# Transposed gathers by DMA from ScalarE, and VectorE's low parts moved in the attention steps

## Chip, cores and metric

One core of a Trainium2 chip runs the whole kernel as one program. The metric is device time in microseconds (us) of one execution; several executions are timed and their median is given. TensorE is called PE, VectorE DVE, ScalarE ACT, GpSimd POOL and SyncE SP, as in the profile.

## What is computed

Linear attention over 8 batches, 8 heads, 576 positions and 64 dimensions, with features exp(±(x·w_phi − max)), followed by two mixture-of-experts layers over the 4608 token rows of 512 numbers, each row going to one of 8 experts:

```python
num = np.einsum('bhsf,bhfd->bhsd', q_p, kv)
den = np.einsum('bhsf,bhf->bhs', q_p, z)[..., None] + 1e-06
...
e_idx = np.argmax(logits, axis=1)
...
h = np.maximum(x[mask] @ w1[e], 0.0)
out[mask] = gate_w[mask, None] * (h @ w2[e])
```

The second layer does the same with other weights and a sigmoid factor on its output.

## The kernel before

Float32 numbers are carried as two float16 parts, a high part `hi` and a low part `lo` (the rest), so that matrix products of float32 quality run as three float16 products on PE. ACT usually makes the high part, DVE the low part.

**Order.** The program is written for a manual schedule: each engine runs its instructions in the order of the Python code. Small chains of DVE work (`Weave`) are put in between, a few steps at each call of `weave.step`.

**Attention.** The loop over `t` has 9 steps for each of the 8 batches, and 6 more; a step is `t % 9`. The work of different batches and heads is staggered: `at(lag)` gives the (batch, index) that began `lag` steps earlier. A step projects keys and queries (PE), takes maxima `km` and `nm` and the difference `kd` (DVE, L1319, L1276, L1325), makes exponentials (ACT, L1334, L1405), the products `kv` (PE, L1348) and `num` (PE, L1433), and normalizes `num` into `xt` (`norm`, DVE, L1413 to L1417), which frees the PSUM bank of `num`. For each finished batch the rows of the next layer are written tile by tile: `x_hi` (ACT, L1515) one step, `x_lo` (DVE, L1520) the step after, `a_T` (PE, L424, eight transposes into the bank `px`, the first four of the high part), `x_logits` and a table entry (`x_enter`, L405, and `tab_out`, L410). Beside this `split0` splits the weights of the first block: `load`, `mx`, `scale`, `hi` (ACT, L249), `lo` (DVE, L258) and `store`, each set down for a step number by `job`; `split_step(split, weave, t, what)` runs all jobs of a kind up to `t`.

**Experts.** `run` is a generator over 80 tiles of 128 rows, 40 of the first block and 40 of the second. For each tile a gather (POOL, `gather`, L788) brings its rows from DRAM to one of four buffers `xg`; `x_T` transposes them, `first` is the first layer in two halves (PE, L818 to L820), `hidden` makes its high part (ACT, L829) and low part (DVE, L830), `second` is the second layer (PE, L840 to L842). In the first block the result `y` of the tile is then scaled (`y_max`, `y_scale`), split (`y_hi` on ACT, L887; `y_lo` on DVE, L892), transposed on PE (`y_T`, L424, copied by ACT at L902) and routed for the second block. The weights of the second block are split meanwhile (L229, L233, L249, L258).

**Transposes of gathered rows.** `x_T(n, i, pe)` has two ways. With `pe` it is eight transposes on PE into a PSUM bank (L424, `px` or `pl` `<-ident,xg`) and a copy to `xT` (`x_T_out`, L807, by ACT at the end of a step). Without, it is one DMA transpose (L800), issued by SP at the top of the step. Which way is taken is set in `run` for the tile two ahead: `soon` is true for all tiles of the first block, so these go to PE, and most of the second block's take the DMA. `lazy` puts PE's transposes behind those of `y` near the end of the step.

**From attention to experts.** `tiles()` advances `run` by one stage. At the end of the attention a few stages are drawn in among the last table entries. When the last entry is in, `route_a` and `route_b` compute on DVE which expert's rows stand in which tile; the gathers of the fourth tile and later need that.

Of the kernel before, what the change touches and what calls it, by code (L numbers as in the profile page):

```python
# [23 lines left out]
B, H, S, D = 8, 8, 576, 64  # L24
# [18 lines left out]
E = 3  # L43
# [13 lines left out]
def attention_two_moe(  # L57
# [6 lines left out]
    nc = tc.nc  # L64
# [85 lines left out]
    def done(chain):  # L150

        while True:
            try:
                next(chain)
            except StopIteration as e:
                return e.value
# [137 lines left out]
    def split_step(split, weave, t, what):  # L294

        if what == "scale":
            split.chains = [weave.add(c) for c in split.go(t, what)]
        else:
            if what == "hi":
                for c in split.chains:  # L300
                    weave.finish(c)
            split.go(t, what)
# [119 lines left out]
    def transposes(ps, parts):  # L422
        for i, a in enumerate(parts):
            nc.tensor.transpose(ps[:, i, :], a, ident16)  # L424
# [15 lines left out]
    def view(t, dt, start, *dims):  # L440
        a = t.bitcast(dt) if dt != F32 else t
        n = int(np.prod(dims))
        names = "abcd"[: len(dims)]
        return a[:, start : start + n].rearrange(
            f"p ({' '.join(names)}) -> p {' '.join(names)}", **dict(zip(names[1:], dims[1:])))
# [18 lines left out]
    xTb = [view(xT_m[i], F16, 0, 8, 128) for i in range(2)]  # L464
# [313 lines left out]
    def xg(n, i):  # L778
        return xgb[(i + state.get("shift", 0)) % 4]
# [12 lines left out]
    def pt():  # L792
        state["pts"] += 1
        return bank(state["pt"][state["pts"] % len(state["pt"])], F16, 8, 128)

    def x_T(n, i, pe=False):

        hl = xg(n, i)[:, 0:DM].bitcast(F16)
        if not pe:
            nc.sync.dma_start_transpose(out=xTb[i % 2], in_=hl)  # L800
            return
        xTp[n, i] = pt()
        transposes(xTp[n, i], [hl[:, 128 * k : 128 * k + 128] for k in range(8)])
# [177 lines left out]
    def run(seq):  # L981
# [3 lines left out]
        head = seq[0][1] == 0  # L985

        def at(u):
            return seq[u] if 0 <= u < n0 else None
# [40 lines left out]
        for u in range(n0 + 3):  # L1029
            cur, nxt_ = at(u), at(u + 1)  # L1030
# [10 lines left out]

            pre = head and cur and cur[1] == E - 1

            soon = pre or cur and head and at(u + 2) and at(u + 2)[0] == 0

            turn = head and at(u + 2) and at(u + 2)[0] == 1 and at(u + 2)[1] < 2
            if at(u + 2) and known(u + 2) and not soon and not turn:
# [31 lines left out]
            elif old2:  # L1079
                i = old2[1]  # L1080
# [88 lines left out]
    with ExitStack() as actx:  # L1169
# [14 lines left out]
        weave = Weave()  # L1184

        split0 = Splitter(0, stage0, parts_of(*xg_m, *xT_m), sm, ((), ()), 32, 3, 7, junk=acc.tile([128, 1024], F8, name="junk"))
# [299 lines left out]
        def x_of(b, c):  # L1486
            return xts[b][:, c] if c < 4 else xrs[b // 2]
# [30 lines left out]
        def x_lo(b, c):  # L1518
            hl = row(b, c)[:, 0:DM].bitcast(F16)
            nc.vector.scalar_tensor_tensor(  # L1520
                out=hl[:, DM : 2 * DM], in0=x_of(b, c), scalar=rows[b, "s"][:, c : c + 1], in1=hl[:, 0:DM],
                op0=ALU.mult, op1=ALU.subtract)
# [60 lines left out]
        def x_hots(b):  # L1583
            n = 4 + b % 2
            if b < B - 2:
                areas = [wop.tile([128, 1024], F32, tag="wo", name="wo")]
            else:
                areas = [io.tile([128, 4, 2, F], F32, tag="kprem", name="kprem", bufs=1).rearrange("p a b c -> p (a b c)")]
            mems = []
            for a in areas:  # L1590
                a = a if a.dtype == F16 else a.bitcast(F16)
                mems += [a[:, 416 * i : 416 * i + 416] for i in range(a.shape[1] // 416)]
            mems = mems[0:4]
            if n == 5:
                mems.append(wk.tile([128, 8, 128], F16, tag="xT", name="xT", bufs=1).rearrange("p a b -> p (a b)")[:, 0:416])
            at_ = []
            pk, po = rows.pop((b, "pk"))
            yield from hots(at_, pk, po, codes[0][:, 9 * (b // 2) + 4 * (b % 2) :], mems)
            rows[b, "hots"] = at_[0]

        def x_enter(b, tag="qf"):
            rows[b, "pt"] = tab_add(tag, rows.pop((b, "hots")))
# [22 lines left out]
        def tiles():  # L1625
            if not chains.get("route"):
                chains["route"] = next(experts)

        chains = {}
        for t in range(9 * B + 6):  # L1630
            b, s = t // 9, t % 9

            def at(lag, n=9):

                u = t - lag
                return (u // 9, u % 9) if 0 <= u < 9 * B and u % 9 < (n if n else 4 + u // 9 % 2) else None
# [15 lines left out]
            def end(lag, name):  # L1652
                if at(lag, 1):
                    weave.finish(chains.pop((name, at(lag, 1)[0])))

            if 9 <= t < 18 or t >= 9 * B - 14:
                next(zeros_, None)
            if t == 4:
# [61 lines left out]
                    done(q_parts(0))  # L1720
                weave.step()
            done(norm_)
            if at(17, 0) and at(17)[0] < B - 1:
                x_lo(*at(17))
            each(6, x_max)
            weave.step()

# [35 lines left out]
            split_step(split0, weave, t, "hi")  # L1763
            weave.step(2)
            weave.step()
            split_step(split0, weave, t, "lo")
            if entered is not None:
                tab_out(0, rows.pop((entered, "pt")))
            weave.step()
# [60 lines left out]
        x_store(last)  # L1830
        done(x_places(last))
        done(x_hots(last))
        x_enter(last, "num2")
        tab_out(0, rows.pop((last, "pt")))

# [89 lines left out]
```

## Time and profile before

| | us |
|---|---|
| median of 3 runs | 1468.89 |
| range of these | 1467.31 to 1476.05 |
| the profiled execution | 1468.27 |
| its span in the trace | 1466.4 |

The profiled execution has a span from the first to the last instruction; times in the trace count from its start. "Busy" is the time in which an engine had an instruction running. Matmuls overlap each other, so the distance between the starts of two is what one costs in a full PE. "Idle before <- releaser" says how long an engine stood before an instruction, and what ended the wait. The granted clock is 1.00 at 2.4 GHz and 0.50 at 1.2 GHz.

### The profile page before, as it was taken

How to read it: one execution, taken by the hardware profiler on the slowest of the kernel's cores; microseconds unless marked ns; L12 is line 12 of the kernel's file. 1: busy time of each engine (PE TensorE's matmuls, PEld its weight loads, DVE VectorE, ACT ScalarE, POOL GpSimd, SP SyncE). 2: the span in 40 equal slices, each digit the busy share in tenths (PEclk: the TensorE clock that was granted, in tenths of full speed). 3: DMA queues.
4: the chain of work that ended last, by engine and by line, in shares of the span. 5: the costliest groups of instructions: out<-in, count | busy, mean ns of one | idle time of the engine just before them, and what ended most of it. 6: DMA issues, size and time to landing. Idle time of an engine off the chain costs nothing. (4 is left out here: it accounts for less than half of the span.)

```text
span 1466.4 us, 40153 instructions
## 1 busy us (share of the span) xinstructions
PE 1407.8 (96%) x16132; PEld 1146.3 (78%) x16132; DVE 852.2 (58%) x2579; ACT 649.7 (44%) x1010; POOL 159.4 (11%) x208
## 2 busy tenths in 40 slices
PE   6999999999899998999999999999999999999997
PEld 4999888989889896777777777777676777777775
DVE  3688888887887757687777877775611111111110
ACT  1467666666657541456565555643211111111111
POOL 1000000000000000111111111011121212121211
PEclk8999999999898888999999999999999999999999
DMA  7367767768563272466667665789454262773470
GB/s 232 130 207 260 245 195 244 217 215 242 200 206 132 112 290 81 122 231 235 224 214 239 228 224 198 228 309 368 168 143 129 77 192 68 231 240 95 128 248 32
DMA packets 157681, 285.31 MB, mean 195 GB/s; under 512 B 85657, under 2 KB 86573, under 8 KB 150320
## 3 DMA queue, kind: packets, MB, share of 16 engines
q1 hardware_dynamic: 143104, 241.10, 50.6%
q0 software_dynamic: 12352, 41.40, 8.6%
q8 instruction: 130, 2.13, 0.6%
q14 instruction: 63, 0.52, 0.1%
q10 hardware_dynamic: 2032, 0.16, 0.1%
HBM read 444.04 MB, written 98.63 MB: 370 GB/s over the span
## 5 line engine op out<-in xcount | busy, mean ns | idle before, releaser
L830 DVE SCALAR_TENSOR_TENSOR qs<-proj,qs 128x512 f16<-128x512 f32 x107 | 73.6, 688 | 246.3 <-ACT qs L829 245.6
L818 PE MATMUL proj<-xT,w 128*128 128x128 f16 x896 | 154.1, 220 | 0.0
L819 PE MATMUL proj<-xT,w 128*128 128x128 f16 x896 | 154.0, 220 | 0.0
L820 PE MATMUL proj<-xT,w 128*128 128x128 f16 x896 | 154.0, 220 | 0.0
L1433 PE MATMUL num<-kvsb,E 128*128 128x65 f32 x1024 | 130.3, 283 | 10.4 <-DVE xt L1417 9.6
L819 PE MATMUL proj<-xT,v 128*128 128x128 f16 x816 | 138.7, 219 | 0.1
L820 PE MATMUL proj<-xT,v 128*128 128x128 f16 x816 | 138.7, 219 | 0.0
L818 PE MATMUL proj<-xT,v 128*128 128x128 f16 x816 | 138.7, 219 | 0.0
L1348 PE MATMUL kv<-v,kp 128*128 128x128 f32 x1024 | 138.4, 292 | 0.0
L1433 PEld LDWEIGHTS num<-kvsb,E 128*128 128x128 f32 x1024 | 126.4, 201 | 13.1 <-issue 7.8
L818 PEld LDWEIGHTS <-w 128*128 128x128 f16 x1344 | 132.4, 99 | 2.0
L819 PEld LDWEIGHTS <-w 128*128 128x128 f16 x1344 | 132.4, 99 | 2.0
L820 PEld LDWEIGHTS <-w 128*128 128x128 f16 x1344 | 132.4, 98 | 0.0
L1348 PEld LDWEIGHTS kv<-v,kp 128*128 128x128 f32 x1024 | 129.5, 205 | 0.4 <-issue 0.4
L841 PE MATMUL num<-w,qs 128*128 128x512 f16 x336 | 127.3, 379 | 0.0
L842 PE MATMUL num<-w,qs 128*128 128x512 f16 x336 | 127.3, 379 | 0.0
L840 PE MATMUL num<-w,qs 128*128 128x512 f16 x336 | 127.3, 379 | 0.0
L829 ACT ACTIVATE qs<-proj 128x512 f16<-128x512 f32 x107 | 63.5, 594 | 141.1 <-PE proj L820 138.0
L842 PEld LDWEIGHTS <-qs 128*128 128x128 f16 x640 | 62.6, 98 | 75.5
L819 PEld LDWEIGHTS <-v 128*128 128x128 f16 x1216 | 118.9, 98 | 2.5 <-issue 0.3
L818 PEld LDWEIGHTS <-v 128*128 128x128 f16 x1216 | 118.9, 98 | 2.1
L820 PEld LDWEIGHTS <-v 128*128 128x128 f16 x1216 | 118.9, 98 | 0.0
(358 smaller groups left out, 3636.0 us busy)
## 6 DMA issues: line engine op xcount, KB each, us to landing
w<-pl SPq DMA_DIRECT2D x152, 1024.0 KB
v<-pl SPq DMA_DIRECT2D x80, 1024.0 KB
ks<-pl SPq DMA_DIRECT2D x80, 1024.0 KB
pl<-wo SPq DMA_DIRECT2D x66, 512.0 KB
w<-in_moe_w_dram SPq DMA_DIRECT2D x64, 512.0 KB
wf<-in_moe_w_dram SPq DMA_DIRECT2D x64, 512.0 KB
pl<-qs SPq DMA_DIRECT2D x26, 512.0 KB
ks<-in_k_dram SPq DMA_DIRECT2D x16, 576.0 KB
```

The costliest lines, as they stand in the source:

```text
L818: nc.tensor.matmul(h[:, j], wk[:, 0, cs], xT[:, k], start=(k == 0), stop=False)
L819: nc.tensor.matmul(h[:, j], wk[:, 0, cs], xT[:, 4 + k], start=False, stop=False)
L820: nc.tensor.matmul(h[:, j], wk[:, 1, cs], xT[:, k], start=False, stop=(k == 3))
L829: nc.scalar.activation(out=hi, in_=h, func=AF.Relu)
L830: nc.vector.scalar_tensor_tensor(out=lo, in0=h, scalar=0.0, in1=hi, op0=ALU.max, op1=ALU.subtract)
L840: nc.tensor.matmul(y, h[:, 0, k], wk[:, 0], start=(k == 0), stop=False)
L841: nc.tensor.matmul(y, h[:, 0, k], wk[:, 1], start=False, stop=False)
L842: nc.tensor.matmul(y, h[:, 1, k], wk[:, 0], start=False, stop=(k == 7))
L1348: nc.tensor.matmul(ps[:, half, h % 2], kp[:, c, half, :], vw(v1, 4 * h + c), start=(h % 2 == 0 and half == 0 and c == 0), stop=False)
L1433: nc.tensor.matmul(ps[:, c, 0:V], e[:, half, 128 * c : 128 * c + 128], kw(g, half), start=(half == 0), stop=(half == 1))
```

## The change

Gathered rows are transposed by DMA in the first block too, from tile 6 on (the seventh); every DMA transpose is now issued by ACT in place of SP. In an attention step `x_lo` is called at the top, ahead of all else, in place of after `done(norm_)`. The split's `lo` jobs are run at the top of the next step in steps without an `x_hi`, and where they were in the others. Before the last table entry one more stage of the experts is drawn.

```diff
-            nc.sync.dma_start_transpose(out=xTb[i % 2], in_=hl)
+            nc.scalar.dma_start_transpose(out=xTb[i % 2], in_=hl)
...
-            soon = pre or cur and head and at(u + 2) and at(u + 2)[0] == 0
+            soon = pre or cur and head and at(u + 2) and at(u + 2)[0] == 0 and at(u + 2)[1] < E + 3
...
+            if at(17, 0) and at(17)[0] < B - 1:
+                x_lo(*at(17))
+            split_step(split0, weave, t - 1, "lo")
             if 9 <= t < 18 or t >= 9 * B - 14:
                 next(zeros_, None)
...
             done(norm_)
-            if at(17, 0) and at(17)[0] < B - 1:
-                x_lo(*at(17))
             each(6, x_max)
...
-            split_step(split0, weave, t, "lo")
+            if not (at(16, 0) and at(16)[0] < B - 1):
+                split_step(split0, weave, t - 1 if t < 9 * B + 5 else t, "lo")
+            else:
+                split_step(split0, weave, t, "lo")
...
         done(x_hots(last))
+        tiles()
         x_enter(last, "num2")
```

On ACT, one tile of the first block before, from the high part of y (L887) on; `wf` are weights of the second block, `px` and `pl` PSUM banks, numbers behind a name tell buffers apart:

```order
L887 ACTIVATE qs_146<-num_7448,cs 128x512
L829 ACTIVATE qs_147<-kv 128x512
L249 ACTIVATE wo<-wf_6790,sb 128x1024
L233 ACTIVATE junk,wmx<-wf_6791 128x1024
L829 ACTIVATE qs_147<-proj 128x512
L902 COPY xT_144<-px 128x1024
L807 COPY xT_143<-pl 128x1024
L249 ACTIVATE qs_145<-wf_6790,sb 128x1024
L233 ACTIVATE junk,wmx<-wf_6791 128x1024
L887 ACTIVATE rw_6786<-num,cs 128x512
```

The same tile on ACT now:

```order
L887 ACTIVATE qs_146<-num_7448,cs 128x512
L829 ACTIVATE qs_147<-kv 128x512
L249 ACTIVATE wo<-wf_6859,sb 128x1024
L233 ACTIVATE junk,wmx<-wf_6860 128x1024
L829 ACTIVATE qs_147<-proj 128x512
L902 COPY xT_144<-px 128x1024
L800 DMA_TRANSPOSE xT_144<-xg_142 128x8x128
L249 ACTIVATE qs_145<-wf_6859,sb 128x1024
L233 ACTIVATE junk,wmx<-wf_6860 128x1024
L887 ACTIVATE rw_6855<-num,cs 128x512
```

The copy of the gathered rows' transposes (L807) went, and the DMA transpose (L800) stands in its place, ahead of the next tile's L249, L233 and L887. There are 34 more DMA transposes than before, and SP has none.

On DVE, an attention step with an `x_lo` (L1520, `rows_f<-xt`), before, from the split's low part of the step ahead to that of this step:

```order
L258 SCALAR_TENSOR_TENSOR xT_144<-w_1_153,sb,xT_144 128x1024
L1413 TENSOR_SCALAR den<-num 128x4
L1415 RECIPROCAL den<-den 128x4
L1319 TENSOR_REDUCE km<-proj 128x4
L1417 TENSOR_TENSOR xt<-num,den 128x4x64
L1276 TENSOR_REDUCE nm<-proj 128x4
L1325 TENSOR_TENSOR kd<-proj,km 128x512
L1520 SCALAR_TENSOR_TENSOR rows_f<-xt,sb,rows_f 128x512
L229 TENSOR_REDUCE wmx<-w_0_152 128x1
L258 SCALAR_TENSOR_TENSOR wo<-w_0_154,sb,wo 128x2x512
```

The same step on DVE now:

```order
L258 SCALAR_TENSOR_TENSOR xT_144<-w_1_153,sb,xT_144 128x1024
L1520 SCALAR_TENSOR_TENSOR rows_f<-xt,sb,rows_f 128x512
L1413 TENSOR_SCALAR den<-num 128x4
L1415 RECIPROCAL den<-den 128x4
L1319 TENSOR_REDUCE km<-proj 128x4
L1417 TENSOR_TENSOR xt<-num,den 128x4x64
L1276 TENSOR_REDUCE nm<-proj 128x4
L1325 TENSOR_TENSOR kd<-proj,km 128x512
L229 TENSOR_REDUCE wmx<-w_0_152 128x1
L258 SCALAR_TENSOR_TENSOR wo<-w_0_154,sb,wo 128x2x512
```

`x_lo` moved ahead of six instructions, those that normalize `num` and read the projections.

On DVE at the end of the attention, where the last one-hot rows (L396) are followed by the table add (L410), the start of `route_a` (L668, L671) and the scaling of a tile's y (L870 to L892), before:

```order
L396 TENSOR_SCALAR xT<-iota_c,po 128x288
L410 TENSOR_TENSOR tab_94<-tab_94,num_6762 96x384
L668 TENSOR_TENSOR v_0_150<-nxt_111,row_115 128x8
L671 TENSOR_TENSOR v_0_150<-v_0_150,iota_t 128x288
...
L870 TENSOR_TENSOR c<-xg_141,efac_169 128x1
L872 TENSOR_REDUCE mx<-num 128x1
```

The same place now:

```order
L396 TENSOR_SCALAR xT<-iota_c,po 128x288
L870 TENSOR_TENSOR c<-xg_141,efac_169 128x1
L872 TENSOR_REDUCE mx<-num 128x1
...
L892 SCALAR_TENSOR_TENSOR qs_146<-num,cs,qs_146 128x512
...
L830 SCALAR_TENSOR_TENSOR qs_145<-kv,qs_145 128x512
L410 TENSOR_TENSOR tab_94<-tab_94,num_6831 96x384
L668 TENSOR_TENSOR v_0_150<-nxt_111,row_115 128x8
```

The scaling and splitting of that y and one low part of a hidden layer (L830) now stand ahead of the table add and the routing.

## Rows read from the trace of the kernel before

**Rows 1.** Page, part 2: granted clock of PE in 40 equal slices.
```profile
PEclk8999999999898888999999999999999999999999
```

**Rows 2.** Windows of the attention and the first block: us, busy by engine, clock, DMA, GB/s.
```profile
core 0: us, PE busy (x) PEld busy (x) DVE busy (x) ACT busy (x) POOL busy (x), PEclk, DMA share, GB/s
100.00:545.00 445.00, 417.34 (x4548) 395.21 (x4547) 353.20 (x934) 285.58 (x473) 15.45 (x20) 0.91 0.65 213
603.00:1041.00 438.00, 437.86 (x5492) 332.94 (x5490) 321.55 (x1117) 237.73 (x333) 51.68 (x63) 1.00 0.70 240
```

**Rows 3.** Timeline of PE in the first block: start us, us, instruction; four tiles apart.
```profile
780.24 0.38 PE L840 MATMUL num<-w,qs 128*128 128x512 f16 x1
...
803.28 0.61 PE L424 MATMUL px<-ident,qs 128*128 128x128 f16 x8
803.73 0.61 PE L424 MATMUL pl<-ident,xg 128*128 128x128 f16 x8
804.17 0.38 PE L840 MATMUL num<-w,qs 128*128 128x512 f16 x1
...
827.57 0.38 PE L840 MATMUL num<-w,qs 128*128 128x512 f16 x1
```

**Rows 4.** Gathers in mid-block and at its end, DMA transposes: times to landing, of issue.
```profile
DMA to landing us min/median/max: 3.8/5.4/6.4
...
xg<-x_d,eidx POOLq DMA_INDIRECT x3, 8.0
...
L800 SPq DMA_TRANSPOSE xT<-xg x36: 1244/1261/3014, 1033.6 to 1427.5; - x36
```

**Rows 5.** Timelines of POOL, ACT, DVE and PE in one tile of the first block.
```profile
851.22 1.03 POOL L788 DMA_INDIRECT xg<-x_d,idx  x1 [10.01 <-PE pl L424]
...
853.39 1.03 ACT L807 COPY xT<-px 128x1024 f16<-128x1024 f16 x1
854.29 1.18 ACT L249 ACTIVATE qs<-wf,sb 128x1024 f16<-128x1024 f32 x1
...
859.23 0.69 ACT L887 ACTIVATE qs<-num,cs 128x512 f16<-128x512 f32 x1 [2.73 <-DVE cs L881]
...
860.50 0.74 DVE L892 SCALAR_TENSOR_TENSOR qs<-num,cs,qs 128x512 f16<-128x512 f32 x1
...
862.24 0.22 PE L424 MATMUL pl<-ident,qs 128*128 128x128 f16 x1
```

**Rows 6.** Waits of PE (100 to 545 us) and DVE (100 to 500): total, times, longest.
```profile
PE num L1433 <- DVE xt L1417: 9.0, 11, 1.7
PE px L424 <- DVE rows_f L1520: 8.3, 5, 2.2
...
PE px L424 <- DVE pb L192: 4.1, 2, 2.0
...
DVE km L1319 <- PE proj L1256: 45.6, 35, 2.4
```

**Rows 7.** Timelines of DVE and PE in the attention step shown above.
```profile
195.81 0.15 DVE L1413 TENSOR_SCALAR den<-num 128x4 f32<-128x4 f32 x1
...
196.67 0.41 DVE L1417 TENSOR_TENSOR xt<-num,den 128x256 f32<-128x256 f32 x1
...
198.20 0.74 DVE L1520 SCALAR_TENSOR_TENSOR rows_f<-xt,sb,rows_f 128x512 f16<-128x512 f32 x1
...
199.00 0.61 PE L424 MATMUL px<-ident,rows_f 128*128 128x128 f16 x4 [2.21 <-DVE rows_f L1520]
```

**Rows 8.** Windows of 4 us behind four such waits, columns as in rows 2.
```profile
200.00:204.00 4.00, 4.00 (x24) 3.87 (x25) 1.74 (x5) 2.02 (x3) 0.00 (x0) 0.50 0.40 116
268.00:272.00 4.00, 4.00 (x28) 3.64 (x29) 2.12 (x7) 1.61 (x3) 0.00 (x0) 0.50 0.68 215
332.00:336.00 4.00, 4.00 (x29) 3.64 (x29) 2.26 (x7) 2.80 (x6) 0.91 (x1) 0.50 0.50 133
464.00:468.00 4.00, 4.00 (x22) 3.93 (x21) 3.82 (x6) 3.19 (x6) 0.00 (x0) 0.50 0.00 0
```

**Rows 9.** Timeline of PE where attention ends and the first block begins.
```profile
569.10 0.26 PE L405 MATMUL num<-kprem 128*96 128x128 f16 x1 [2.11 <-DVE kprem L396]
...
590.40 0.29 PE L424 MATMUL px<-ident,xg 128*128 128x128 f16 x2 [0.22 <-DMA xg<-x_d,idx]
```

## Prediction

> **What bounds the kernel now.** I read the page's busy shares and slices first, then the windows by stage, PE's waits in each stage, and last the timelines of one tile and of one attention step. The page's line of granted clocks has an 8 in slice 1, then in slices 11 and 13 to 16 (of 36.7 us each), and 9 from there on [rows 1]. The windows [rows 2] split that. In the attention (100 to 545 us) PE is busy 417 of 445 us, but at a mean clock of 0.91, while DVE is busy 79% and ACT 64%. In the first mixture-of-experts block (603 to 1041 us) PE is busy 437.86 of 438 us at clock 1.00: there only work taken from PE shortens anything. In that stretch the list of PE's waits is empty.
>
> A tile of the first block shows what is in it [rows 3]: 8 transposes of y begin at 803.28, 8 of the gathered rows (px or pl<-ident,xg) at 803.73, the second layer at 804.17. Four tiles take 827.57 − 780.24 = 47.33 us, 11.83 each.
>
> **The change part by part.**
>
> *1. Transposes leave PE.* From tile 6 to tile 39 of the first block, 34 tiles lose their 8 transposes: 804.17 − 803.73 = 0.44 us each [rows 3], since in a full PE the start-to-start time is the price, not the 0.61 us that the row shows. 34 × 0.44 = 15.0 us. The Trainium skill (TensorE: Matmul & The Clock Gate, Part 4) gives about 275 ns for a transpose within a kernel, 2.2 us a tile; by it 75 us would go. The rows disagree: eight fit between 803.73 and 804.17, 55 ns each, and the sum keeps these.
>
> *2. ACT issues the transfer.* ACT loses a 1.03 us copy of the transposed rows (PSUM to SBUF) and gets the issue of a DMA transpose. No row shows one on ACT; on SP it took 1.244 to 3.014 us, median 1.261 [rows 4]. I take 1.26: about +0.2 us on an engine that is not full. The new thing is a wait: the issue stands in ACT's order at the top of the step, right behind the copy of y's transposes, and needs the gather of that tile to have landed. Queued behind it are two operations for the second block's weights (L249, L233) and then y_hi (L887), on which y_lo on DVE and then PE's transposes of y wait.
>
> Is the gather late? One tile [rows 5]: the gather starts at 851.22, and one takes 3.8 to 6.4 us to landing, median 5.4 [rows 4], so 856.6. ACT comes to that place at 853.39, stands 3.2 us, issues until 857.9, then needs the 2.2 us from 854.29 to 856.50 (2.73 before 859.23) for L249 and L233: 860.1 against y_hi at 859.23. It counts 0.44 more, as PE reaches the next tile that much earlier: 1.3 us late. Two covers: DVE starts y_lo only at 860.50, so y_hi (0.69) may be about 0.6 late; and y_lo ends at 861.24, 1.0 before PE's transposes of y at 862.24. 1.6 of cover for 1.3: nothing is lost. With the slowest gather, 6.4, 0.7 is. ACT idles 2.73 in this tile; over the stretch it is 438 − 237.7 = 200 us [rows 2], 5.4 for each of some 37 tiles, so the other three of a group of four have more. One tile in four may lose up to 0.7, 8 times: 0 to +6, I take +1. It cannot gain.
>
> *3. The DMA engines.* They are 0.70 busy in this stretch at 240 GB/s [rows 2], which makes 343 when full; 128 × 1024 two-byte numbers are 0.26 MB, estimated at 0.8 us of all engines, 0.07 of a tile. Free room is 0.30, and the transposed rows are needed a step later. I take 0. The Trainium skill (Trainium Kernel Development and Optimization, Key Constraints) says that DMAs of all queues share the 16 engines and another issuer saves only issue time. By it the transfer's 0.8 us would still be 0 here with 0.30 free, and a loss where the engines are full; that case is a rival below.
>
> *4. The second block* already had its transposes as transfers, from SP; all come from ACT now, 36 that ran [rows 4]. SP loses that issue. ACT issues at the top of a step, when the gather has long landed and the next hidden layer is 48 matmuls of 55 ns away, 2.65 us. 0; at most a few tenths either way.
>
> *5. x_lo first in the attention step.* PE's waits there [rows 6]: 8.3 us in 5 plus 4.1 in 2 for a step whose second four transposes of a rows tile (L424) need x_lo (L1520), 12.4 us in 7, one a batch. (The two put down to pb are the same: x_lo ends beside it.) In the one shown [rows 7] x_lo starts at 198.20, behind six instructions of DVE, and PE goes on at 199.00. Now x_lo starts where den did, 195.81, and ends by 196.55; PE has its transposes done by about 197.2. What is late next is xt (L1417), which frees the bank that the following num matmuls write: 196.67 + 0.41, and now 0.74 later, so 197.8. A wait of 0.6 to 0.7 stays of 2.2. 7 × 0.7 = 5 of 12.4 remain: −7.5. Bounds: −12.4 (all goes), and 0 (xt later takes it all).
>
> *6. The clock.* Behind that wait the granted clock is 0.50 from 200 to 204: 1.2 in place of 2.4 GHz. The same stands behind those of three other batches, at 268, 332 and 464 us [rows 8]. Each such stretch is some 7 us long, so it costs about 3.4 us; 4 × 3.4 = 13.6. As a wait of 0.7 stays in the same step, I count half as gone: −7. Bounds 0 and −13.6.
>
> *7. x_lo in the other steps, and low parts of the weights a little later.* The 24 other x_lo steps of the seven batches put 0.74 us ahead of km and xt. DVE waits 45.6 us for PE before km in 100 to 500 us, 35 times [rows 6], so in most steps x_lo fills that gap. Where it does not, num's wait for xt (9.0 us in 11) grows. The split's low parts only move past a few short operations. I take +3, bounds −3 to +8.
>
> *8. One more stage of the experts ahead of the last table entry.* The wait of 2.11 us at 569.10 is filled with 2.65 us of matmuls. But the table add and the routing chain now stand behind y_max, y_lo and one hidden low part on DVE, and their end releases the gather for which PE waits 0.22 at 590.40 with no slack [rows 9]. So only what the moved work finds of idle DVE time ahead of the table add comes through. −1, between −2.1 and, if the chain ends later, +2.
>
> **Sum.** −15.0 + 1 − 7.5 − 7 + 3 − 1 = −26.5. The profiled execution took 1468.27 us (span 1466.4 and 1.9 around it), 0.6 under the median of three, 1468.89. 1468.3 − 26.5 = 1441.8, as a median about 1442.
>
> **The rivals.**
>
> A. *The attention gives nothing*: xt takes over x_lo's wait and the clock falls as before. For it: DVE is 79% busy, and num already waits for xt 11 times. Against: DVE's 45.6 us of idle time. Then −15 + 1 − 1: 1453.5.
>
> B. *The transfers become the bound* of the first block: were the engines full, each would push the weights by 0.8 us, 34 × 0.8 = +27. For it: 0.70 is a mean, and the weights come in bursts; against: it leaves 0.30 free. 1468.3 − 15 + 27 − 12.5 = 1468, no change.
>
> C. *ACT stands too long behind the gather*, slower than before. The three gathers at the stage's end took 8.0 us [rows 4]. At 8.0 the tile of rows 5 gets y_hi at 862.7, 3.5 late, 3.9 with the shift, 2.3 beyond its cover. The other three of a group have about 2.4 us more idle and two of them thinner cover; I work them at 0.5 to 1.5, mean over the four 1.3. 34 × (1.3 − 0.44) = +29, less 12.5 from the attention: 1485. It decides from a landing of about 7.3 us on, where 0.8 us a tile eats everything. Against: no gather in mid-block took over 6.4.
>
> D. *The clock stays up wherever x_lo was late*: all of 12.4 and 13.6 goes: 1468.3 − 15 + 1 − 26 − 1 = 1427.
>
> **How the numbers follow.** Forecast 0.64, A 0.20, B 0.05, C 0.06, D 0.05. A measurement of this kernel can tell about 1% from no change; 1% under the median is 1454.2. A lies on that line: a little over half below, as its own bounds go down further than up. Faster: 0.64 + 0.05 + 0.11 = 0.80; same: 0.09 + 0.05 = 0.14; slower: 0.06. The range goes from 1426, by D with a gain in part 7, to 1458, A with the full +6 of part 2.
>
> **What would show it.** In the profile after: no px or pl<-ident,xg from the seventh tile on, four tiles in about 45.6 us (−1.77), PE's waits in 603 to 1030 still empty, a DMA transpose on ACT of about 1.3 us, ACT idle before it for the gather by 1 to 4 us, y_hi later but y's transposes not waiting. In the attention: 7 waits at L424 gone, waits of about 0.7 at L1433 behind them, mean clock 0.93 or 0.94. Wrong it would be if PE waits for y_lo at L424 in the first block (C), for weights at L818 or L840 (B), or if the attention is as long as before (A).

## The result, and the profile after

The changed kernel takes 1481.41 us (median of 20 runs, 1472.54 to 1493.27) against 1464.41 us before (20 runs, 1457.47 to 1476.05): a ratio of 1.0113, 95% interval [1.0091, 1.0135]. It is slower by 1.1%, where 1442 and faster was forecast. The profiled execution has a span of 1477.5 us against 1466.4.

The two halves of the change came out apart, one far better than forecast and the other far worse. To see it, the span is cut at the starts of tiles: a tile starts with the first of its second layer's 24 matmuls (L840, as the first and last line of [rows 3]). The starts are numbered from 0 in the trace's order, and two tiles whose second layers follow each other closely share one: start 1 is that of the second and third tile, start 40 that of two tiles of the second block. So start 2 belongs to the fourth tile, and start 39 to the first tile of the second block. "Tile 2" or "tiles 2 to 39" in the expectations and below mean these starts.

| stretch, us | before | after | difference |
|---|---|---|---|
| beginning to start 0 (attention, change-over) | 561.42 | 532.30 | −29.1 |
| start 0 to 2 | 41.80 | 40.16 | −1.6 |
| start 2 to 39 (first block) | 437.75 | 468.08 | +30.3 |
| start 39 to 41 (change of block) | 37.76 | 45.62 | +7.9 |
| start 41 to the end (second block) | 387.67 | 391.34 | +3.7 |

First the page's line of clocks and the windows, columns as in [rows 2]. The second window ends at start 0.

```profile
PEclk9999999999999799999999999999999999999999
```

```profile
100.00:545.00 445.00, 426.01 (x4896) 400.51 (x4895) 372.90 (x1018) 291.33 (x484) 15.13 (x22) 0.95 0.68 220
100.00:532.30 432.30, 413.92 (x4758) 391.76 (x4757) 363.21 (x968) 289.32 (x480) 14.65 (x20) 0.94 0.68 222
603.00:1041.00 438.00, 404.72 (x4862) 300.28 (x4860) 305.37 (x1055) 190.89 (x274) 48.09 (x58) 0.98 0.79 248
```

The same stretch of before, 100 us to start 0:

```profile
100.00:561.42 461.42, 431.44 (x4761) 408.35 (x4760) 364.00 (x968) 291.21 (x481) 15.45 (x20) 0.90 0.64 208
```

In the attention, 11.6 of the 29.1 us are idle time gone (461.42 − 431.44 = 30.0 against 18.4), and 17.5 are busy time of PE that shrank with the same instructions in it: the clock, 0.90 to 0.94. The dips in slices 11 to 16 of [rows 1] are gone; one 7 remains.

In the first block PE is idle 33.3 us of 438 where it was idle 0.14, at clock 0.98. Its waits, and ACT's (total, times, longest), 600 to 1040 us:

```profile
PE qf L429 <- ACT xT L902: 17.8, 7, 3.6
PE px L424 <- DVE rw L892: 5.3, 4, 1.4
PE pl L424 <- DVE qs L892: 4.1, 3, 1.4
PE kv L818 <- DMA w<-pl: 1.5, 1, 1.5
...
ACT wo L249 <- issue: 52.5, 9, 8.9
ACT os L934 <- issue: 40.0, 8, 5.5
ACT junk L233 <- DMA wf<-in_moe_w_dram: 39.9, 7, 6.6
...
ACT qs L249 <- issue: 23.0, 5, 7.0
```

PE never waits for the transposed rows. It waits for y_lo (L892) at y's transposes, and for ACT's copy of them (L902), each time behind a late ACT. ACT waits, 115.5 us in 22, for "issue" ahead of L249 and L934, the instructions that stand right behind the transfer. The name means that no finished instruction explains the wait; the timelines of four tiles do: in 26 of 31 tiles ACT issues the transfer within 0.2 us of the landing of that tile's gather. First POOL, ACT, DVE:

```profile
750.02 1.03 POOL L788 DMA_INDIRECT xg<-x_d,idx  x1 [9.85 <-DVE gs L316]
...
763.62 1.06 POOL L788 DMA_INDIRECT xg<-x_d,idx  x1 [4.59 <-DVE po L373]
774.74 1.02 POOL L788 DMA_INDIRECT xg<-x_d,idx  x1 [10.06 <-DVE c L914]
...
789.51 1.03 POOL L788 DMA_INDIRECT xg<-x_d,idx  x1 [11.91 <-DVE val L896]
```

```profile
755.05 1.52 ACTq L800 DMA_TRANSPOSE xT<-xg  x1
756.62 0.20 ACT L934 ACTIVATE os<-os 128x4 f32<-128x4 f32 x1 [4.75 <-issue]
...
760.78 0.69 ACT L887 ACTIVATE qs<-num,cs 128x512 f16<-128x512 f32 x1 [0.48 <-DVE cs L881]
...
770.37 1.25 ACTq L800 DMA_TRANSPOSE xT<-xg  x1
771.66 1.15 ACT L249 ACTIVATE wo<-wf,sb 128x1024 f16<-128x1024 f32 x1 [6.88 <-issue]
772.72 0.67 ACT L887 ACTIVATE qs<-num,cs 128x512 f16<-128x512 f32 x1
...
780.50 1.06 ACT L233 ACTIVATE junk<-wf 128x1024 fp8e5<-128x1024 f32 x1 [5.59 <-DMA wf<-in_moe_w_dram]
780.75 1.36 ACTq L800 DMA_TRANSPOSE xT<-xg  x1
...
782.03 1.00 ACT L902 COPY xT<-pl 128x1024 f16<-128x1024 f16 x1
```

```profile
756.85 0.17 DVE L936 TENSOR_SCALAR os<-os 128x4 f32<-128x4 f32 x1 [3.00 <-ACT os L934]
...
762.48 0.74 DVE L892 SCALAR_TENSOR_TENSOR qs<-num,cs,qs 128x512 f16<-128x512 f32 x1
...
773.61 0.74 DVE L892 SCALAR_TENSOR_TENSOR qs<-num,cs,qs 128x512 f16<-128x512 f32 x1
```

Read them as one chain: gather at 763.62, landed when L800 starts at 770.37; ACT, which was idle for 6.88 us up to L249 (the last 1.29 are the issue), goes on with L249 and y_hi (772.72); y_lo on DVE (773.61); and when its last reads of the old row buffer are done (L895, L896), the next gather starts, 774.74. Then it begins again. The stand makes the gather late, and the late gather makes the next stand. PE's own work for four tiles, without the transposes, is 45.55 us, 11.4 for each. The plain round, 763.62 to 774.74, takes 11.12 and would still fit. The rounds beside it do not: 13.60 us from 750.02, where the gate's L934 stands behind the transfer and DVE waits 3.00 us for it, and 14.77 from 774.74 to the next gather at 789.51, where ACT waits 5.59 us for the weights `wf`.

Those weights are late by a second path. SP's loads wait for ACT's transfers, too, which they never did before; the sum in 600 to 1030 us, and SP's issues around the transfer of 770.37:

```profile
SPq L482 <- DMA xT<-xg: 116.1, 18, 11.4
```

```profile
762.73 1.15 SPq L262 DMA_DIRECT2D pl<-qs  x1
773.62 0.61 SPq L482 DMA_DIRECT2D v<-pl  x2
...
775.33 0.40 SPq L222 DMA_DIRECT2D wf<-in_moe_w_dram  x1
```

The load at 773.62 had waited for a semaphore (a counter on which engines wait) that the transfer raises when it lands, so it stood behind a transfer that ACT had not even issued; `wf` went out after it. PE's largest wait, L429 for ACT's copy (17.8 us in 7), comes each time right behind one of ACT's seven waits for `wf`. In PE's timeline:

```profile
739.04 0.38 PE L840 MATMUL num<-w,qs 128*128 128x512 f16 x1
...
783.09 0.27 PE L429 MATMUL qf<-wg,xT 128*128 128x32 f16 x4 [2.38 <-ACT xT L902]
...
790.71 0.38 PE L840 MATMUL num<-w,qs 128*128 128x512 f16 x1
```

Four tiles in 51.67 us, against 47.33 in [rows 3].

### The profile page after: what moved, and what is told of

The parts are those of the page before. It is cut to its first block, busy times and chain, and to the rows that moved or that the text cites. A ratio compares the mean times of both kernels' runs of the same rounds, so it can differ in the third digit from the quotient of the medians.

```text
span 1477.5 us, 39657 instructions
## 1 busy us (share of the span) xinstructions
PE 1389.0 (94%) x15860; PEld 1120.1 (76%) x15860; DVE 852.9 (58%) x2579; ACT 616.4 (42%) x976; POOL 158.6 (11%) x208
## 5 line engine op out<-in xcount | busy, mean ns | idle before, releaser
L830 DVE SCALAR_TENSOR_TENSOR qs<-proj,qs 128x512 f16<-128x512 f32 x107 | 73.7, 689 | 273.1 <-ACT qs L829 273.1
L818 PE MATMUL proj<-xT,w 128*128 128x128 f16 x896 | 155.6, 221 | 7.0 <-SPq L1858 4.8
L819 PE MATMUL proj<-xT,w 128*128 128x128 f16 x896 | 155.6, 221 | 0.0
L820 PE MATMUL proj<-xT,w 128*128 128x128 f16 x896 | 155.6, 221 | 0.0
L818 PE MATMUL proj<-xT,v 128*128 128x128 f16 x816 | 144.0, 223 | 1.3 <-DMA v<-pl 1.3
L819 PE MATMUL proj<-xT,v 128*128 128x128 f16 x816 | 143.9, 223 | 0.0
L820 PE MATMUL proj<-xT,v 128*128 128x128 f16 x816 | 143.7, 223 | 0.0
L1433 PE MATMUL num<-kvsb,E 128*128 128x65 f32 x1024 | 127.7, 279 | 11.7 <-DVE xt L1417 11.5
L1433 PEld LDWEIGHTS num<-kvsb,E 128*128 128x128 f32 x1024 | 122.9, 196 | 16.0 <-issue 9.7
L1348 PE MATMUL kv<-v,kp 128*128 128x128 f32 x1024 | 133.3, 285 | 0.0
L840 PE MATMUL num<-w,qs 128*128 128x512 f16 x336 | 128.6, 383 | 0.4 <-DVE tab L410 0.4
L842 PE MATMUL num<-w,qs 128*128 128x512 f16 x336 | 128.8, 383 | 0.0
L841 PE MATMUL num<-w,qs 128*128 128x512 f16 x336 | 128.6, 383 | 0.0
L1348 PEld LDWEIGHTS kv<-v,kp 128*128 128x128 f32 x1024 | 124.2, 198 | 0.5 <-issue 0.3
L818 PEld LDWEIGHTS <-v 128*128 128x128 f16 x1216 | 120.9, 99 | 3.6 <-DMA v<-pl 1.5
L819 PEld LDWEIGHTS <-v 128*128 128x128 f16 x1216 | 120.8, 99 | 2.1
L820 PEld LDWEIGHTS <-v 128*128 128x128 f16 x1216 | 120.9, 99 | 0.0
```

What stands on the lines that cost most here:

```text
L818: nc.tensor.matmul(h[:, j], wk[:, 0, cs], xT[:, k], start=(k == 0), stop=False)
L819: nc.tensor.matmul(h[:, j], wk[:, 0, cs], xT[:, 4 + k], start=False, stop=False)
L820: nc.tensor.matmul(h[:, j], wk[:, 1, cs], xT[:, k], start=False, stop=(k == 3))
L830: nc.vector.scalar_tensor_tensor(out=lo, in0=h, scalar=0.0, in1=hi, op0=ALU.max, op1=ALU.subtract)
L840: nc.tensor.matmul(y, h[:, 0, k], wk[:, 0], start=(k == 0), stop=False)
L841: nc.tensor.matmul(y, h[:, 0, k], wk[:, 1], start=False, stop=False)
```

## The experiments

All are timed against the kernel before on the same chip. Ratio with 95% interval; the stretches are those of the table above, from each kernel's trace.

| kernel | us, median | ratio | to start 0 | 0 to 2 | 2 to 39 | 39 to 41 | 41 to end |
|---|---|---|---|---|---|---|---|
| attn_only | 1435.97 | 0.9812 [0.9777, 0.9846] | 530.77 | 40.06 | 437.75 | 37.88 | 387.24 |
| xlo_first_only | 1440.96 | 0.9841 [0.9805, 0.9878] | 532.53 | 41.81 | 437.75 | 37.82 | 388.09 |
| xlo_and_tiles | 1438.82 | 0.9820 [0.9792, 0.9848] | 532.60 | 40.12 | 437.75 | 37.89 | 388.54 |
| transposes_only | 1507.60 | 1.0264 [1.0210, 1.0317] | 560.52 | 43.04 | 473.22 | 44.31 | 390.71 |
| xT_after_yhi | 1474.42 | 1.0087 [1.0038, 1.0135] | 528.53 | 40.04 | 464.46 | 41.56 | 389.61 |
| xT_on_SP | 1434.25 | 0.9793 [0.9760, 0.9827] | 530.42 | 40.07 | 437.45 | 37.83 | 387.23 |
| gather_early_ACT | 1454.31 | 0.9919 [0.9881, 0.9956] | 531.49 | 40.18 | 438.21 | 48.46 | 393.36 |
| ACT_stands_only | 1441.64 | 0.9824 [0.9791, 0.9856] | 536.37 | 40.23 | 440.43 | 37.95 | 387.42 |
| ACT_stands_1us | 1450.07 | 0.9897 [0.9869, 0.9925] | 536.28 | 40.02 | 448.94 | 37.74 | 387.32 |
| SP_and_ACT_stands | 1462.70 | 0.9981 [0.9955, 1.0007] | 533.98 | 40.09 | 461.69 | 37.86 | 387.28 |
| ACT_first_SP_second | 1473.27 | 1.0053 [1.0028, 1.0078] | 528.95 | 40.02 | 475.22 | 37.84 | 387.37 |
| PE_first_ACT_second | 1449.39 | 0.9879 [0.9832, 0.9925] | 531.99 | 40.17 | 437.75 | 45.03 | 391.76 |
| late_SP | 1430.22 | 0.9765 [0.9728, 0.9801] | 533.29 | 40.11 | 430.01 | 37.90 | 387.39 |
| gather_early_SP | 1424.76 | 0.9725 [0.9690, 0.9761] | 531.84 | 40.04 | 426.82 | 37.77 | 387.83 |
| best_SP_39_on_PE | 1425.35 | 0.9737 [0.9704, 0.9769] | 533.52 | 40.21 | 423.01 | 37.69 | 387.47 |
| best_lateSP_39_on_PE | 1425.56 | 0.9740 [0.9707, 0.9773] | 530.36 | 40.20 | 425.32 | 37.72 | 387.70 |
| attn_gather_early | 1436.99 | 0.9807 [0.9779, 0.9836] | 531.50 | 40.39 | 437.76 | 37.97 | 387.98 |

The first column of stretches scatters: the kernels with the same attention code in all three edits have start 0 at 528.5 to 536.4, so a difference of a few us there says nothing. The first block of the changed kernel scatters as well: ACT_first_SP_second, which does not touch it, took 475.22 there against 468.08.

### The two halves apart

attn_only is the changed kernel with the transposes as before:

```diff
-            nc.scalar.dma_start_transpose(out=xTb[i % 2], in_=hl)
+            nc.sync.dma_start_transpose(out=xTb[i % 2], in_=hl)
...
-            soon = pre or cur and head and at(u + 2) and at(u + 2)[0] == 0 and at(u + 2)[1] < E + 3
+            soon = pre or cur and head and at(u + 2) and at(u + 2)[0] == 0
```

Expected: 

> The three attention edits alone (x_lo at the head of the step, lo after the next step's head, the extra tiles() before the last rows), the first block's transposes on PE and the second block's on SyncE as before. If the 30.8 us between the starts of tile 2 belong to these edits (603.22 before, 572.46 after), the time falls to about 1464 - 29 = 1435 us, ratio 0.980, and tiles 2 to 39 take 437 to 440 us. Rival: part of the gain was made by other things (the freed PE banks, ACT's order), then 1445 to 1455.

transposes_only is the kernel before with just these two lines the other way. Expected: 

> The transposing transfers alone, attention as before. If the whole loss (30.3 us in tiles 2 to 39, 7.9 at the change of block, 3.7 in the second block) is theirs, 1464 + 42 = 1506 us, ratio 1.029. Rival: part of the loss comes from the earlier attention end (colder loads of the extra experts, other phase of the steps), then 1480 to 1495.

Measured: 1435.97 and 1507.60. Both first readings hold, and the halves add up within their intervals: −30 and +41 make +11, where the whole change measured +17.

### The attention's gain

xlo_first_only is the kernel before with x_lo moved to the head of the step; xlo_and_tiles has the added tiles() too.

```diff
+            if at(17, 0) and at(17)[0] < B - 1:
+                x_lo(*at(17))
             if 9 <= t < 18 or t >= 9 * B - 14:
...
             done(norm_)
-            if at(17, 0) and at(17)[0] < B - 1:
-                x_lo(*at(17))
```

Expected: 

> The kernel before with x_lo at the head of the attention step alone. My forecast priced it at -7.5 us and the clock with it at -7; all three attention edits gave -30. If x_lo is the core of it: -20 to -28 us (ratio 0.981 to 0.986), PE's waits for L424 gone from the attention stage and its clock at 0.94 to 0.95. If the deferral of lo or the additional tiles() step carries half of it: -8 to -15 us.

Expected: 

> x_lo at the head of the step and the additional tiles() step, lo undeferred. x_lo alone brought tile 0 to 532.53 and left 41.81 us from there to tile 2; all three edits brought 530.77 and 40.06. If the additional tiles() step makes the second difference: tile 0 near 532.5, tile 2 some 40 us later, whole about 1439; if the deferral of lo makes both: as x_lo alone, 1441.

Measured: 1440.96 with x_lo alone, −25.5 us of the −30, inside the first reading's −20 to −28; 1438.82 with the stage, as expected (1439). With x_lo alone, the attention up to start 0, and PE's longest waits from 100 to 545 us:

```profile
100.00:532.53 432.53, 413.50 (x4748) 391.74 (x4749) 361.45 (x966) 289.33 (x479) 15.19 (x20) 0.94 0.68 222
...
PE num L1433 <- DVE xt L1417: 12.5, 16, 1.7
PE px L405 <- DVE wo L396: 2.8, 12, 0.4
```

The L424 waits of [rows 6] are gone, the wait for xt grew from 9.0 to 12.5 us as forecast, and the whole gain is there: idle time 30.0 to 19.0, busy time 431.44 to 413.50. The added tiles() makes start 0 to 2 shorter by 1.7 us (41.81 to 40.12). What lo's deferral brings (1438.82 against 1435.97) is inside the intervals and stays open.

### The first block: is it ACT's stand?

xT_after_yhi moves the issue behind y_hi, where the gather has mostly landed; xT_on_SP gives it to SP at the same place; gather_early_ACT leaves it on ACT and reads the old row buffer earlier, so that the gather can be moved from the end of the step to a place ahead of y_hi.

```diff
 xT_after_yhi, in run()
                 done(c)
                 y_hi(old[1])
+            if late_x and known(u + 2) and not soon and not turn:
+                x_T(*at(u + 2))
 gather_early_ACT: L895, L896 moved from y_lo to y_max, and in run()
                 c = y_scale(old[1])
+                if known(u + 3):
+                    gather(*at(u + 3))
                 next(c)
```

Expected: 

> The changed kernel with one line moved: in the first block ACT issues the transposing transfer of tile u+2 behind y_hi of the step in place of at its head, when the gather has mostly landed; same transfers, same queue, same bytes. Theory 1 (ACT stands in order behind the gather): ACT's idle time ahead of L249 and L934 goes, four tiles take about 45.6 us in place of 51, tiles 2 to 39 about 425 to 432 us and the whole about 1481 - 40 = 1441 us (1435 to 1450). Theory 2 (the transposing traffic itself delays loads and gathers): four tiles stay at 50 to 51 us and the whole at 1475 to 1485.

Expected: 

> The changed kernel with SyncE as the issuer of the transposing transfers in both blocks, at the same place in the order. Theory 1: ACT no longer stands, but SyncE does, with weight loads behind it; tiles 2 to 39 fall to 428 to 445 us, the change of block and the second block return to before's 37.8 and 387.7 us: 1435 to 1455 us. Theory 2 (traffic): the first block stays near 468 us, whole 1470 to 1480. Theory 3 (ACT's own queue lands transposes late): only the last two stretches return, -11 us.

Expected: 

> The changed kernel, ACT still issuing at the head of the step, with the two reads of the old row buffer taken from y_lo to y_max, so that the gather of tile u+3 may start some 3 to 4 us earlier in each step. If what holds ACT is that it stands in order until the gather has landed (L800 starts 5.0 to 6.8 us behind the gather, and y_hi, y_lo and the next gather stand behind it), the loop opens: ACT's idle time put down to issue ahead of L249 and L934 (115 us in 22 waits between 600 and 1030) falls below 30 us, tiles 2 to 39 fall from 468 to 432 to 445 us, the whole to 1445 to 1458. Rival (the transposing transfers need 10 to 13 us to land wherever they start, and that is what PE waits for): no gain, 1475 to 1485, with PE waiting for xT.

xT_after_yhi, 1474.42, fits neither theory: the time is nearly that of theory 2, but ACT's stands are gone, and PE now waits where it had not: in 600 to 1030 us

```profile
PE proj L818 <- DMA xT<-xg: 15.2, 5, 4.5
PE kv L818 <- DMA xT<-xg: 11.6, 4, 4.5
```

One of the nine, the issue on ACT, PE's wait that it ends, and the windows while the transfer is in flight and behind the wait:

```profile
796.58 2.45 ACTq L800 DMA_TRANSPOSE xT<-xg  x1
```

```profile
809.27 0.27 PE L818 MATMUL proj<-xT,w 128*128 128x128 f16 x1 [4.46 <-DMA xT<-xg]
```

```profile
797.00:809.00 12.00, 7.81 (x76) 4.88 (x73) 11.45 (x35) 4.97 (x7) 1.07 (x1) 0.91 1.06 189
809.30:813.30 4.00, 4.00 (x39) 4.00 (x40) 1.39 (x7) 0.00 (x0) 1.03 (x1) 0.50 1.04 168
```

PE had the rows 12.69 us after the issue, more than a tile later. This is one of the slow ones: by the DMA packets of the trace, half of the run's first-block transfers end within 4.9 us of their issue, and the slowest take 12.3; in the changed kernel they take 2.6 to 7.7. The DMA engines were full at 189 GB/s, while part 3 of the forecast had worked out 343 for full engines. And behind the wait of 4.46 us PE ran at half clock. So the changed kernel's place at the head of the step has a reason: from there the transfer lands in time, but ACT stands; from behind y_hi ACT is free, but some transfers are late.

xT_on_SP, 1434.25, is theory 1's, just under its range: SP stands in place of ACT (70.2 us in 28), and PE waits for xT only twice, 4.9 us. This one edit, the issuer, takes 47 us from the changed kernel. But its 437.45 us for tiles 2 to 39 are what attn_only takes with the transposes on PE; the 15 us that they leave free have not come. gather_early_ACT, 1454.31, opens the loop at its other end, as its first reading has it: ACT's "issue" waits in 600 to 1030 fall from 115.5 us in 22 to 9.2 in 9, of which ahead of L249

```profile
ACT wo L249 <- issue: 5.2, 6, 1.3
ACT qs L249 <- issue: 4.0, 3, 2.7
```

and tiles 2 to 39 take 438.21 in place of 468.08. SP's loads still wait for ACT's transfers there, 66.6 us in 13, and here too the 15 us are missing. The rest of its loss stands at the change of block and in the second block (48.46 and 393.36).

### Stand, issue or traffic

ACT_stands_only and ACT_stands_1us have no transfer in the first block (transposes on PE); SP_and_ACT_stands has xT_on_SP's transfers. In each an ACT operation on the gathered rows stands at the head of the step:

```diff
+            if cur and head and at(u + 2) and at(u + 2)[0] == 0 and at(u + 2)[1] >= E + 3:
+                st = sp.tile([128, 1], F32, tag="st", name="st")
+                nc.scalar.copy(st, xg(*at(u + 2))[:, 0:1])
 ACT_stands_1us, in place of the last two:
+                nc.scalar.activation(out=state["split"].junk, in_=xg(*at(u + 2))[:, 0:DM].bitcast(F16), func=AF.Copy, saturate=False)
```

Expected: 

> No transfer at all: the attention edits, the first block's transposes on PE, and at the head of the step, where the changed kernel has the transfer, ACT copies one column of the gathered rows of tile u+2 into a scratch tile (34 copies). It makes ACT stand in order behind the gather and nothing else. Theory 1 (the stand and the loop through y_hi, y_lo and the next gather): tiles 2 to 39 take 455 to 470 us in place of 437.75, the whole 1455 to 1470. Theory 2 (the transfers' traffic): as the attention edits alone, 1436 to 1439 with some 0.2 us per copy on ACT.

Expected: 

> As ACT_stands_only, but the 34 operations read all 1024 columns of the gathered high parts and take about 1.0 us each on ACT, behind the stand, as long as the issue of a transfer holds ACT there (1.25 us). No transfers in the first block. If the loop gather, stand, ACT's next work, y_hi, y_lo, next gather is what sets the period, four more us per four tiles go straight into it: four tiles near 50 us, whole 1455 to 1472. If the traffic is the missing half: 1443 to 1447.

Expected: 

> SyncE issues the transfers at the head of the step and ACT copies one column of the gathered rows there: stand and traffic, but no issue on ACT. If the traffic (wf and the transposes landing late) turns the stand into the loss: 1455 to 1472. If the issue on ACT does: 1434 to 1443.

The first was a miss: theory 1 as I had put it wanted 455 to 470 us for tiles 2 to 39, and 440.43 came, 2.7 over attn_only (the whole, 1441.64, is over theory 2's 1439). Standing alone nearly fits under PE's 437.75. With 1 us of ACT work behind each stand it is 448.94 (1450.07, between the two readings): 8.5 us for 34 us of work, not four in four tiles. With SP's transfers it is 461.69 (1462.70, the first reading), and with ACT as issuer, as in the change, 468.08 (475.22 in ACT_first_SP_second). The last two have 15 us less to do on PE, so what they lose is 39 us and 45 to 52. The stands themselves, for the same copy, without and with SP's transfers:

```profile
ACT st L1049 <- DMA xg<-x_d,idx: 92.9, 32, 6.4
```

```profile
ACT st L1049 <- DMA xg<-x_d,idx: 138.0, 32, 8.7
ACT junk L233 <- DMA wf<-in_moe_w_dram: 31.3, 14, 5.2
```

2.9 and 4.3 us each; and with the transfers, ACT also waits for the split's loads. But SP_and_ACT_stands adds more than traffic: SP itself stands at the gather, with the weight loads behind it, 81.7 us in 32.

So the stand alone costs little, and far more with transfers beside it. How much of that is traffic on the DMA engines and how much are weight loads held up in SP's order, behind its own stand or behind ACT's transfers, these runs do not separate. The traffic alone is not the loss: with the same transfers from SP and the gather early, tiles 2 to 39 take 426.82 (gather_early_SP).

### The change of block, and the second block

ACT_first_SP_second is the changed kernel with SP as issuer in the second block alone, PE_first_ACT_second is attn_only with ACT there.

```diff
-            nc.scalar.dma_start_transpose(out=xTb[i % 2], in_=hl)
+            (nc.scalar if n == 0 else nc.sync).dma_start_transpose(out=xTb[i % 2], in_=hl)
```

Expected: 

> The changed kernel with SyncE as issuer in the second block, ACT still in the first. If the second block's issuer makes the 7.9 us at the change of block and the 3.7 us behind it: 1481 - 11.6 = 1470. If the change of block is late because of the first block's own disorder (late rows, late weights): only the 3.7 us return, 1477.

Expected: 

> The attention edits, the first block's transposes on PE, and ACT as issuer of the second block's transfers. By the first reading 1436 + 11.6 = 1448; by the second 1436 + 3.7 = 1440, with single waits of 1 to 1.5 us for xT in the second block.

The first brings 39 to 41 back to 37.84 and the rest to 387.37; its median, 1473.27, lies between the two readings, and the first block of its trace came out 7 us longer; so the stretches decide. The second, 1449.39 and with an undisturbed first block, has 45.03 and 391.76, as the first reading says. Both say that the issuer there makes the 11.5 us. In PE_first_ACT_second the transfer for the third tile, and PE's wait for it:

```profile
1002.33 1.35 ACTq L800 DMA_TRANSPOSE xT<-xg  x1
```

```profile
1019.50 0.26 PE L818 MATMUL proj<-xT,w 128*128 128x128 f16 x1 [4.14 <-DMA xT<-xg]
```

17.17 us from the issue to PE's start, beside the second block's first weights. In the changed kernel the same transfer, issued at 1032.95, has its last packet 17.2 us later, and PE waits 4.84 us there; from SP's queue (xT_on_SP, issued at 1000.65) the last packet comes 4.9 us behind the issue. Further on single transfers cost waits of up to 0.9 us here, and 1.5 in the changed kernel:

```profile
1208.92 0.22 PE L818 MATMUL kv<-xT,w 128*128 128x128 f16 x1 [1.48 <-DMA xT<-xg]
```

Why the same transfer lands so much sooner from SP's queue is not shown.

### Towards a faster kernel

late_SP places SP's issue behind y_hi in program order; gather_early_SP is xT_on_SP with the early gather; the two "best" add the first block's last tile (number 39 in the kernel's count) on PE to the early gather, with SP's issue at either place; attn_gather_early is the control without transfers in the first block.

```diff
-            soon = ... and at(u + 2)[1] < E + 3
+            soon = ... and (at(u + 2)[1] < E + 3 or at(u + 2)[1] == NMAIN - 1)
```

Expected: 

> SyncE issues the transposing transfers, placed behind y_hi in program order, so that the step's first weight loads stand ahead of them in SyncE's queue. SyncE gets there when those loads are issued, not when ACT is done with y_hi. If only the issuer counts (ACT's y_hi is late, SyncE is early): as good as at the head of the step on SyncE, 1428 to 1438 us. If a place further down means a late landing whichever the issuer, PE waits for xT as with ACT behind y_hi: 1455 to 1475.

Expected: 

> SyncE as issuer at the head of the step, and the gather early as in the run before. SyncE then stands less and the splitting loads behind it come earlier: ACT's 41.2 us of waits for wf (15 times) shrink, PE's waits for ACT's copy of yT (5.0 us in 6) and for xT (4.9 us in 2) go, four tiles come near 45.6 us: 1420 to 1430 us, the best so far. Rival: SyncE's stand is hidden already, 1432 to 1437 as without.

Expected: 

> The early gather with SyncE as issuer, and tile 39, whose transfer met the second block's weight loads (issued at 952.19, landed 14.62 us later, PE waiting 2.48), transposed on PE as the first tiles are. If that one tile is what kept the stretch from four tiles in 45.55 us, tile 36 to 37 of the trace falls from 16.0 to about 12, and the whole from 1424.8 to about 1421 us. Rival: the wait passes to another tile or to the weights, 1424 to 1426.

Expected: 

> The same with SyncE's transfers behind y_hi in program order. With the gather early both places give 45.55 us per four tiles, so the same time within 2 us: 1419 to 1424.

Expected: 

> The attention edits and the early gather, the first block's transposes all on PE: the control for what the transposes' leaving PE is worth. If the early gather only serves the transfers, nothing changes against the attention edits alone (1436, ratio 0.981), and the 11 us between that and 1424.8 are the transposes gone from PE (my forecast's first term, -15). If an earlier gather is worth something by itself: 1428 to 1433.

gather_early_SP, 1424.76, is 2.75% under before (0.9725 [0.9690, 0.9761]) and the best that was run; the two "best" kernels are not to be told from it. Its PE, starts 21 and 25:

```profile
787.74 0.38 PE L840 MATMUL num<-w,qs 128*128 128x512 f16 x1
...
833.28 0.38 PE L840 MATMUL num<-w,qs 128*128 128x512 f16 x1
```

45.54 us per four tiles, the forecast's 47.33 − 1.77. The early gather alone gives nothing (1436.99): it only serves the transfers. The last tile on PE takes 3.8 us from the first block in the trace (426.82 to 423.01) and nothing that the medians show: 1425.35, in the rival's 1424 to 1426. With SP's issue behind y_hi it is 1425.56, over the 1419 to 1424 that I expected, but the same within 2 us as it should be. late_SP, 1430.22, has the first reading: from SP the place behind y_hi is as good as the head of the step.

## Why the prediction was wrong

−26.5 us was forecast, and +17.0 came.

**Part 1, transposes leave PE, −15.0: right.** Where nothing stood in the way, 33 tiles without them (best_SP_39_on_PE) took 437.75 − 423.01 = 14.7 us less; 33 × 0.44 is 14.5.

**Part 2, ACT's issue, +1: the step that failed.** It did see that ACT would stand at the gather, with y_hi and y_lo behind it. But it set one tile's lateness against that tile's cover, with the gather at its old time, and followed one path, through y_hi. The gather itself starts when y_lo is done, so lateness comes back as a later gather one tile on; the time to work out was that of the loop, 11.1 to 14.8 us in the rounds shown, against PE's 11.4. It also left out what else stands behind the transfer: L934, for which DVE waits, and SP, which part 4 has only losing an issue, and whose weight loads waited for ACT's transfers for 116.1 us. 30.3 + 15 = 45 us came in place of 1, with part 3's share in it. Of these, 30.6 go with the issuer (468.08 against 437.45 from SP); the rest was lost with SP as issuer, too, and came back only with the early gather (426.82). How the 30.6 divide among the round through y_hi, L934 and SP's late loads stays open: no run takes these apart.

**Part 3, the DMA engines, 0: mis-sized, and the wrong question.** A transfer was priced by its bytes at 0.8 us of all engines. In the changed kernel ACT's queue against SP's, 600 to 1030 us:

```profile
q1 hardware_dynamic: 22496, 76.97, 51.6%
...
q10 hardware_dynamic: 33792, 8.39, 12.6%
```

For 32 transfers: 0.126 × 430 / 32 = 1.7 us each, per byte over twice what the weights take. The Trainium skill (Trainium Kernel Development and Optimization, Key Constraints) says that another issuer only saves issue time. These runs show more: the issuer alone decided between 1434 and 1481 us.

**Part 4, the second block, 0: failed**, +7.9 and +3.7. It looked at ACT's free time and not at when the transfer lands (17.2 us after its issue for the first one).

**Parts 5 and 6, x_lo and the clock, −14.5: right in mechanism, half in size.** x_lo alone: idle time −11.0 where −7.5 stood and the bound was −12.4; busy time −17.9 where the clock was given −7 and the bound was −13.6. The four windows of [rows 8] did not hold all the half-clock time: over 461 us a mean of 0.90 is 46 us lost against full clock, not 13.6; at 0.94 over 432.5 it is still 26.

**Parts 7 and 8, +3 and −1:** the added stage gave −1.7, inside its bounds; num's wait for xt grew by 3.5 us as part 7 has it (9.0 to 12.5), within the −11.0 above; the low parts show neither a loss nor a gain.

**Rivals.** It was C's mechanism, at a landing of about 5.5 us, well under the 7.3 from which C was to decide, because C too was worked out without the loop; and half hidden by an attention that gave D's 26 and more. B did not come: in the first block the DMA engines were 0.79 busy in the mean. "PE's waits empty in the first block" was the sign named for a right forecast; L424's wait for y_lo, the sign named for C, is what came (9.4 us in 7), and beside it a larger one that no rival named, L429's (17.8 in 7).

## What to carry to other kernels

A DMA on a compute engine's queue is an instruction that can wait, and everything behind it waits too: before moving an issue, ask whether its source has landed when the engine gets there, and whether what stands behind it leads back to that source. If it does, work out the loop's period and compare it with the bottleneck's time per tile; cover counted for one tile is spent once. Look at the other queues as well: here SP's weight loads waited for transfers that ACT had yet to issue. A short wait of PE in a dense stretch can be worth more than its length, since the clock behind it is part of its price: with x_lo first, 11.0 us of idle time took 17.9 of busy time with them.

## What was not expected of the hardware

A DMA transpose of 128 × 1024 two-byte numbers within SBUF, 0.26 MB, moved its last packet 2.6 to 7.7 us after its issue in the changed kernel's first block. All packets of the one issued at 770.37, in the window 770.3 to 773.2 us (packets, MB, share of the 16 engines):

```profile
q10 hardware_dynamic: 1056, 0.26, 46.8%
```

Beside other loads it was far slower at times: 12.69 us above, and 17.17 at the change of block. While the first of these ran, the DMA engines were full at 189 GB/s, where the first block before had 240 GB/s at 0.70 [rows 2]. The issue held ACT's stream 1.25 us behind a stand (L800 at 770.37, L249 at 771.66); at 780.75 it ran beside an activation that had begun before it.
